# A written-out instruction sequence for each engine in place of ranked picks, and all bulk weights on one queue

## The chip, the core and the metric

The kernel runs on one core of a Trainium2 chip. What is measured is the device time of one execution, in microseconds (us). The core has five instruction streams that this kernel uses: TensorE (PE, with its weight loads PEld), VectorE (DVE), ScalarE (ACT), GpSimd (POOL) and SyncE (SP), which here only issues DMAs. Every stream runs its instructions strictly in order and waits on semaphores that the others raise.

## The reference

The input x has 2048 tokens of 448 features, in bf16. Two kinds of layer alternate, A, B, A, B, and each adds its result to x:

```python
x = x + _A_ref(_layernorm(x, axis=-1), A_wqkv, A_wo)
x = x + _B_ref(_layernorm(x, axis=-1), B_w_gate, B_w_up, B_w_down)
x = x + _A_ref(_layernorm(x, axis=-1), A_wqkv, A_wo)
x = x + _B_ref(_layernorm(x, axis=-1), B_w_gate, B_w_up, B_w_down)
```

A is attention with 16 heads of 28 features, in which each token sees 8 tokens: itself and those 2, 4 ... 14 places before it. The masked scores go through a softmax, and the result through the weight `wo`. B is a gated layer without a nonlinearity: (x w_gate) * (x w_up), 1792 features wide, and then w_down.

## The kernel before

**Data.** Tokens are taken with even ones first and odd ones second, so that a window of 8 tokens at distance 2 is a window of 8 neighbours. x stays in SBUF as 16 blocks of 128 tokens (`x_sb`). Layer 0 (A) works in five chunks of tokens (256, 512, 512, 512, 256), layer 2 (A) in four of 512, layers 1 and 3 (B) in five each. `SEQ` (line 74) lists the 19 jobs, "A00 A01 B10 A02 ...": the digits are layer and chunk. Later layers start on their first chunks while earlier ones still run.

**One chunk of A.** `ln_chunk` (line 762) makes the layernorm of each block: `bn`, `mv` on VectorE (L772, L774), `lnv`, `rstd` on ScalarE (L775, L777), `xn` on VectorE (L793); then the transpose T, by TensorE and an eviction (L803, L809) in layer 0 and by a DMA transpose from SP (L796) elsewhere. `qk_chunk` (line 863) makes q and k in four units, each with two PSUM banks, and evicts them (QK, L895); a copy of some rows goes through DRAM (`vt`, L904) to give v for four heads, which SP fetches with DMA transposes (VT, L915). `v_group` (line 917) makes the other heads' v. `attn_front` (line 993) makes the scores of two blocks of queries in one burst of 64 short matmuls (S, L1007; four banks), the exponentials on ScalarE (Ex, L1014) and the mask on VectorE (E, L1024). `attn_back` (line 1032) multiplies by v in another burst of 64 (AV, L1044; two banks), evicts (Oc, Oa, L1055, L1059) and normalises (Rs, Rl, R, N, L1069 to L1082). `y_blocks` (line 1086) multiplies by `wo` and adds to x (Y, x, L1099).

**One chunk of B.** `b_chunk` (line 1109) makes 14 units of gate and up (Gps; 14 matmuls each, two banks), evicts the gate on ScalarE (G, L1135), multiplies on VectorE (H, L1138) and then runs the down product (Dd) with another addition to x. The last two blocks have their own form (L1150, L1154), and their result goes out in three DMAs.

**PSUM** has eight banks; the queue of work for TensorE depends on when evictions free them.

**The order.** `Sched.add` (line 158) records every operation with the engines that may run it, an estimate of its time, what it depends on and which banks it takes or frees. `schedule` (line 281) then plays the program through with these estimates: whenever an engine is free, it picks among the operations that are ready by this plan the one with the lowest rank. The ranks are sums of tabled numbers by kind of operation and job (`PR`, `JP`, `XP`, lines 56 to 59, `HEAD_P`, `ATT_P`), with rules on when TensorE changes its tiling and how many banks each layer may hold (`HOLD_*`, `A_CAP`, `B_CAP`). An attention burst may be woven with up to two "strip" steps of a wide matmul that is also ready (lines 389 to 410, L537 in the profile). The plan also has estimates of how TensorE's code arrives (`LINE_T`, line 147). `emit` (line 456) writes each engine's instructions in the order found, with the semaphore waits that they need. The estimates set the order alone; on the chip each instruction runs when its waits are met.

**Loads.** Lines 647 to 660 load x, the q,k weights (four parts, `stg`) and the v weights, on the queues of SP and ACT. `bulk` (line 725) issues the large weights after x blocks 8 to 11 have landed: gate parts on SP and up parts on ACT (784 KB each), then `wo` in four parts and w_down in four, each of the latter waiting for the one before it.

Of the kernel before, what the change touches and what calls it, by code (L numbers as in the profile page):

```python
# [1 line left out]

# [7 lines left out]
S = 2048  # L10
D = 448
H = 16
DH = 28
# [14 lines left out]
MAIN = "R64"  # L28
# [5 lines left out]
HEAD_P = (38742.03, -267021.83, -101071.72, 99463.11, 27200.44)  # L34
HOLD_A = 14413.3
HOLD_BA = 5214.2
HOLD_BB = 9573.3
HOLD_N = 2
# [17 lines left out]
PR = {'wu': -168129.17, 'AV': -10462.61, 'rstd': -35978.42, 'bn': 17812.95, 'N': -10212.21, 'Gps': 180828.64, 'Tps': 27409.69, 'H': -109807.89, 'S': 144044.56, 'VT': 70347.33, 'Ex': 79610.91, 'G': -13543.26, 'xn': -79108.55, 'QK': -38047.91, 'Ddps': 24073.96, 'V': -99754.84, 'x': -42794.27, 'lnv': -73394.18, 'Oc': -92185.76, 'Oa': -11984.14, 'R': 151556.02, 'VVps': -36455.43, 'Yps': 17459.84, 'PW': 63857.07, 'T': -30210.14, 'mv': -55530.81, 'Rs': -97577.45, 'Rl': 77935.78, 'QKps': 68347.44, 'E': 103540.24, 'wqk': -93887.3, 'wqp': 55786.95}  # L56
JP = {'A20': -91058.29, 'B32': 33273.33, 'B34': -254788.12, 'A22': -140282.28, 'B13': -13087.65, 'A21': -140403.13, 'B12': -98678.01, 'A02': 51851.79, 'A03': -34167.99, 'B30': -93145.7, 'B31': 78379.27, 'B10': -36992.85, 'B11': -174975.04, 'A23': -71630.68, 'A04': 3260.23, 'B33': -59282.63, 'A01': -61687.66, 'B14': 99825.17, 'A00': -37201.99}
OFF = {}
XP = {'bn': -95955.38, 'mv': 16148.21, 'lnv': -72635.24, 'rstd': 84849.74, 'xn': -172701.07, 'Tps': 15935.95, 'T': 8483.92, 'QK': 48768.14, 'V': -165679.11, 'E': 31912.32, 'Ex': -27261.18, 'S': 103908.79, 'AV': -35522.85, 'Oc': 78601.92, 'Oa': -68237.35, 'N': 141909.88, 'x': -106916.56, 'VT': 41247.37, 'PW': -72014.64}
VONES_L = 6000.0  # L60
BL = (9000.0, 3500.0, 4000.0)
# [7 lines left out]
SEED = 190  # L69
JITTER = 0  # L70
ATT_P = 71709.67
A_CAP = 6
B_CAP = 6
# [59 lines left out]
class Sched:  # L133
# [13 lines left out]
    LINE_T = ((45000.0, 3500.0), (23000.0, 4600.0), (11000.0, 8500.0), (-1.0, 3500.0))  # L147

    def __init__(self):
        self.ops = []  # L150
        self.ready = {}
        self.fed = [(self.HEAD, 0.0)]
        self.lines = [0.0, 0.0]
        self.npos = 0
        self.met = {}
        self.rng = random.Random(SEED)

    def add(self, engs, ins, est, deps=(), prio=0.0, mode=None, acquire=None, release=(), dma=None, lat=0.0, after=None, selfd=(), tmin=None, alt=()):
# [7 lines left out]
        op.prio += JITTER * self.rng.random() + OFF.get(op.idx, 0.0)  # L166
        for _, k in ins:
            k = k[0] if isinstance(k, list) and k else k
            if isinstance(k, tuple) and k[0] in PR and k[0] != "cross" and not (dma and k[1] == -1):
                op.prio += PR[k[0]] + (XP.get(k[0], 0.0) if k[1] == 0 else 0.0)  # L170
                break
# [40 lines left out]
    def pick_banks(self, req, now):  # L212
# [14 lines left out]
        return cand[:req.n]  # L227

# [52 lines left out]
    def schedule(self):  # L281
# [13 lines left out]
        for op in self.ops:  # L295
# [9 lines left out]
            if not srcs:  # L305
                op.rdy = {x: self.ready_at(op, x) for x in op.engs}
                for e in op.engs:
                    pend[e].append(op)
        left = len(self.ops)
        now = 0.0  # L310
        while left:
            moved = False
            b_ready = any(o.acquire is not None and o.acquire.kind == 1 for o in pend["pe"])
            for e in self.ENGS:
                if free[e] > now + 1e-6:
                    continue
                best = None
                cands = []
                for op in pend[e]:
                    if op.rdy[e] <= now + 1e-6:  # L320
                        cands.append((op.prio, op.idx, op))
                cands.sort()
                a_wait = False
                okay = []
                for *_, op in cands:
                    if op.acquire is not None:
# [954 lines left out]
```

## Time and profile before

| | before |
|---|---|
| median of 3 runs | 390.56 us (389.87 to 390.77) |
| the profiled execution | 392.05 us |
| its span, first to last instruction | 390.3 us |
| busy: PE / DVE / ACT / POOL | 381.5 / 275.9 / 200.8 / 8.3 us |
| granted TensorE clock | 1.000 |
| DMA, mean over the span | 58 GB/s; 258, 263, 210 in the first three of 40 slices |

The profile is of one execution. Busy times count instructions of an engine that were running; a matmul's end is modelled from its size, so that a PE that waits a little between matmuls still looks busy. A "pair" below is two matmuls that use the upper and the lower 64 rows of the array at the same time: most of this kernel's matmuls come so. "Idle before, <- X" names what ended the wait of an engine; "issue" is a wait for nothing that the profile shows. In stretches of time, PE was busy as follows.

```profile
0.00:10.00 10.00, 8.74 (x86) 4.00 (x88) 6.17 (x16) 4.85 (x10) 7.22 (x32) 1.00 0.80 261
10.00:20.00 10.00, 9.38 (x192) 5.76 (x188) 9.77 (x33) 8.15 (x22) 0.00 (x0) 1.00 1.07 266
20.00:30.00 10.00, 9.21 (x279) 6.05 (x282) 7.63 (x23) 9.14 (x20) 1.09 (x6) 1.00 0.66 188
30.00:40.00 10.00, 9.86 (x147) 4.62 (x137) 6.79 (x17) 7.88 (x13) 0.00 (x0) 1.00 0.32 91
40.00:50.00 10.00, 9.05 (x319) 5.07 (x319) 7.14 (x17) 8.71 (x13) 0.00 (x0) 1.00 0.67 128
50.00:60.00 10.00, 8.25 (x207) 7.08 (x209) 8.45 (x18) 8.70 (x16) 0.00 (x0) 1.00 0.22 41
60.00:70.00 10.00, 10.00 (x221) 8.04 (x217) 10.00 (x27) 5.74 (x15) 0.00 (x0) 1.00 0.26 51
70.00:80.00 10.00, 9.18 (x284) 5.74 (x282) 8.04 (x23) 6.83 (x15) 0.00 (x0) 1.00 0.48 62
80.00:390.30 310.30, 307.85 (x4712) 167.41 (x4708) 211.93 (x441) 140.80 (x270) 0.00 (x0) 1.00 0.22 37
```

The columns are: the stretch, its length, busy us (and instructions) of PE, PEld, DVE, ACT and POOL, the granted clock, the DMA share and GB/s.

### The profile page before, as it was taken

The numbers are of one execution on the slowest core, as the hardware profiler recorded it, in microseconds if no ns is written. First come the engines' busy times: TensorE is split into PE (matmuls) and PEld (weight loads), VectorE is DVE, ScalarE is ACT, GpSimd is POOL, SyncE is SP. The second block draws the span as 40 slices with busy tenths as digits, with TensorE's granted clock in tenths as the row PEclk, the third lists the DMA queues.
The fourth block names the chain that finished last, engine by engine and source line by source line (L and its number), as shares of the span: only waits on it lengthen the run. The fifth ranks groups of instructions, "written<-read, shape, count | busy, mean of one in ns | idle before, by whom it ended". The sixth has DMA issues, their size and how long they took to land.

```text
span 390.3 us, 14405 instructions
## 1 busy us (share of the span) xinstructions
PE 381.5 (98%) x6394; PEld 213.8 (55%) x6394; DVE 275.9 (71%) x606; ACT 200.8 (51%) x386; POOL 8.3 (2%) x38
## 2 busy tenths in 40 slices
PE   8999989999999999999999999999999999999997
PEld 3555468554555544544456678545445544544584
DVE  6976789899649798496459965287676875467452
ACT  4797886664506676053544645055642542344150
POOL 7010000000000000000000000000000000000000
PEclk9999999999999999999999999999999999999999
DMA  7973532404302413221150204403230212100201
GB/s 258 263 210 92 131 41 56 58 11 83 41 2 53 61 21 50 49 29 29 22 55 15 41 13 33 82 26 52 37 64 29 40 34 50 50 2 2 51 23 47
DMA packets 54753, 22.50 MB, mean 58 GB/s; under 512 B 44884, under 2 KB 54692, under 8 KB 54692
## 3 DMA queue, kind: packets, MB, share of 16 engines
q1 hardware_dynamic: 53188, 19.24, 25.8%
q10 hardware_dynamic: 1504, 2.35, 2.2%
q8 instruction: 50, 0.82, 0.9%
q14 instruction: 11, 0.09, 0.1%
HBM read 8.54 MB, written 2.71 MB: 29 GB/s over the span
## 4 chain that ended last, share of the span: by engine, by line
PE 93%; ACT 4%; DVE 2%; issue 1%; ACTq 0%; DVEq 0%
PE ps L534 83%; PE ps L1007 3%; PE ps L1044 2%; PE ps L700 2%; PE ps L537 2%; PE ps L1150 1%; ACT qk L895 1%; ACT xnTa L809 1%; ACT E_sb L1014 1%; ACT R_sb L1070 0%; ACT g_sb L1135 0%; DVE oT L1082 0%; ACT O_sb L1055 0%; DVE v_sb L987 0%; DVE R_sb L1069 0%
## 5 line engine op out<-in xcount | busy, mean ns | idle before, releaser
L534 PE MATMUL ps<-xnTb,WGU 64*128 64x512 bf16 (+1 forms) x1942 | 176.8, 333 | 0.8 <-issue 0.8
L534 PEld LDWEIGHTS ps<-xnTb,WGU 64*128 64x128 bf16 x1942 | 94.2, 94 | 72.1 <-issue 1.5
L1135 ACT ACTIVATE g_sb<-ps 128x512 bf16<-128x512 f32 (+1 forms) x140 | 71.1, 511 | 92.9 <-PE ps L534 87.7
L1138 DVE TENSOR_TENSOR hT<-g_sb,ps 128x512 bf16<-128x512 bf16 (+1 forms) x140 | 79.6, 575 | 35.9 <-ACT g_sb L1135 34.0
L534 PE MATMUL ps<-WD,hT 64*128 64x448 bf16 x824 | 81.8, 349 | 0.0
L1099 DVE TENSOR_TENSOR x_sb<-x_sb,ps 128x448 bf16<-128x448 bf16 x62 | 35.9, 616 | 40.9 <-PE ps L534 40.8
L534 PEld LDWEIGHTS ps<-WD,hT 64*128 64x128 bf16 x824 | 39.6, 94 | 36.0
L534 PE MATMUL ps<-xnTa,WQK 64*128 64x512 bf16 (+1 forms) x488 | 51.6, 352 | 0.3 <-ACT xnTa L809 0.2
L1014 ACT ACTIVATE E_sb<-ps 128x1024 bf16<-128x1024 f32 (+1 forms) x36 | 33.7, 981 | 20.9 <-PE ps L1007 20.6
L772 DVE BATCH_NORM_STATS2 st<-x_sb 128x6 f32<-128x448 bf16 x64 | 37.4, 610 | 1.6 <-DMA x_sb<-in_A_x_dram 1.6
L793 DVE TENSOR_SCALAR xn_sb<-x_sb,mv,rstd 128x512 bf16<-128x512 bf16 (+1 forms) x64 | 34.1, 570 | 0.9 <-ACT rstd L777 0.8
L534 PEld LDWEIGHTS ps<-xnTa,WQK 64*128 64x128 bf16 x488 | 22.9, 94 | 20.5 <-ACT xnTa L809 1.1
L895 ACT ACTIVATE qk<-ps 128x1024 bf16<-128x1024 f32 (+1 forms) x30 | 26.9, 923 | 10.5 <-PE ps L534 10.3
L534 PE MATMUL ps<-wo_g,oT 64*128 64x448 bf16 x252 | 29.3, 349 | 0.1
L1024 DVE TENSOR_TENSOR E_sb<-E_sb,MK 128x1024 bf16<-128x1024 bf16 (+2 forms) x40 | 23.7, 608 | 7.2 <-ACT E_sb L1014 7.0
L1082 DVE TENSOR_TENSOR oT<-O_sb,R_sb 128x480 bf16<-128x480 f32 (+3 forms) x36 | 21.6, 627 | 5.2 <-ACT R_sb L1071 4.7
L1055 ACT ACTIVATE O_sb<-ps 128x512 f32<-128x512 f32 (+3 forms) x22 | 11.5, 547 | 26.4 <-PE ps L1044 26.3
L1070 ACT ACTIVATE R_sb<-R_sb 128x480 f32<-128x480 f32 (+1 forms) x34 | 20.0, 601 | 8.6 <-DVE R_sb L1069 8.5
L1069 DVE STREAM_SHUFFLE R_sb<-O_sb 128x480 f32<-128x480 f32 (+1 forms) x34 | 22.3, 696 | 0.0
L534 PE MATMUL ps<-WV,xnTa 64*128 64x336 bf16 (+3 forms) x244 | 21.1, 304 | 0.2
L1071 ACT ACTIVATE R_sb<-R_sb 128x480 f32<-128x480 f32 (+1 forms) x34 | 19.6, 601 | 0.4
L534 PEld LDWEIGHTS ps<-wo_g,oT 64*128 64x128 bf16 x252 | 12.5, 94 | 11.8 <-DVE oT L1082 1.1
(59 smaller groups left out, 190.7 us busy)
## 6 DMA issues: line engine op xcount, KB each, us to landing
out_dram<-x_sb SPq DMA_DIRECT2D x15, 112.0 KB, 1.7
WGU<-in_B_w_up_dram ACTq DMA_DIRECT2D x2, 784.0 KB, 11.5
WGU<-in_B_w_gate_dram SPq DMA_DIRECT2D x2, 784.0 KB, 13.5
x_sb<-in_A_x_dram SPq DMA_DIRECT2D x3, 448.0 KB, 7.1
WD<-in_B_w_down_dram SPq DMA_DIRECT2D x2, 448.0 KB, 3.8
hT<-in_A_wqkv_dram ACTq DMA_DIRECT2D x3, 224.0 KB, 3.5
WD<-in_B_w_down_dram SPq DMA_DIRECT2D x2, 336.0 KB, 3.9
vt<-qk SPq DMA_DIRECT2D x42, 16.0 KB
```

Source lines behind the costliest of these rows:

```text
L534: return lambda E: E.matmul(out(), lhs(), rhs(), start=start, stop=stop)
L772: sc.add("dve", one(lambda E, B=B: E.bn_stats(st6[:, B, :], x_sb[:, B, :]), ("bn", li, B)), 525.0, deps=[("x", li - 1, B)] + ([("xn", li - ...
L793: sc.add("dve", one(lambda E, B=B, dst=dst, src=src: E.tensor_scalar(dst, src, mv[:, B, 0:1], rstd[:, B:B + 1], ALU.subtract, ALU.mult), ( ...
L895: return E.activation(dst, src, ACT.Copy) if hasattr(E, "activation") else E.tensor_copy(dst, src)
L1014: return E.activation(E_sb[:, slot, 2 * hp:2 * hp + 2, 0:w], ps[:, b0:b0 + 2, 0:w], ACT.Exp, scale=SCALE)
L1024: return E.tensor_tensor(e, e, m, ALU.mult)
L1069: sc.add("dve", one(lambda E: E.stream_shuffle(R_sb[:, rs, 0:w], O_sb[:, os_, 0:w], [DH] * 32), ("Rs", li, qb)), dve_est(w) + 100.0, deps= ...
L1070: sc.add("act", one(lambda E: E.activation(R_sb[:, rs, 0:w], R_sb[:, rs, 0:w], ACT.Ln), ("Rl", li, qb)), act_est(w, False), deps=[("Rs", l ...
L1082: return E.tensor_tensor(oT[:, :, a % HALF:a % HALF + z - a], O[:, :, a - tok:z - tok], R_sb[:, rs, 0:w].rearrange("p (h n) -> p h n", h=4 ...
L1099: sc.add("dve", one(lambda E: E.tensor_tensor(x_sb[:, B, :], x_sb[:, B, :], ps[:, bk[w], 0:D], ALU.add), ("x", li, B)), dve_est(D), deps=[ ...
L1135: sc.add("act", one(lambda E, gs=gs, bk=bk: E.activation(g_sb[:, gs, 0:nt], ps[:, bk[0], 0:nt], ACT.Copy), ("G", li, j, fc)), act_est(nt), ...
L1138: sc.add("dve", one(lambda E, gs=gs, bk=bk, fc=fc: E.tensor_tensor(hT[:, fc, hs, 0:nt], g_sb[:, gs, 0:nt], ps[:, bk[1], 0:nt], ALU.mult), ...
```

## The change

`schedule` no longer ranks. A table `ORD` holds, for each engine, the numbers of the operations in the order in which that engine runs them (405 items for PE, 390 for ACT, 563 for DVE, 36 for POOL, 164 for SP); "a+b" is a burst woven with the wide matmul b. The play-through remains, to assign banks and to decide how a woven pair is cut, but it takes each engine's next item as given and waits until it is ready by the plan. The tables of ranks, the holding rules and the caps go. `LINE_T` and the estimated landing times of the weights change; these numbers reach the chip only through which banks are taken.

The computation and its matmuls are the same. Of the copies that ACT and DVE may both run (QK, V, T, Oc and a few others), 28 go from ACT to DVE and 28 from DVE to ACT; POOL takes all eight small weight copies of L717 (six before).

```diff
+    def banks_for(self, item, now):
...
+        given = {e: [tuple(map(int, x.split("+"))) for x in ORD[e].split()] for e in self.ENGS}
+        todo = {e: 0 for e in self.ENGS}
...
-                if best is None:
+                item = [self.ops[i] for i in given[e][todo[e]]]
+                if not all(op in pend[e] and op.rdy[e] <= now + 1e-6 for op in item):
                     continue
+                if not self.banks_for(item, now):
+                    continue
+                todo[e] += 1
...
-                if op.tmin is not None and e == "sp":
-                    gate = [o for o in self.pe_done if o.end + self.PE_LAT <= now and isinstance(o.ins[-1][1], tuple) and o.ins[-1][1] in self.ready]
-                    op.deps.append(gate[-1].ins[-1][1])
...
-    LINE_T = ((45000.0, 3500.0), (23000.0, 4600.0), (11000.0, 8500.0), (-1.0, 3500.0))
+    LINE_T = ((75000.0, 4300.0), (22000.0, 5300.0), (11000.0, 7700.0), (-1.0, 5000.0))
...
+    for j in range(4):
+        dst = wo_g[32 * j:32 * j + DH, :, :]
+        src = A_wo.rearrange("(c j e) d -> j e c d", c=4, j=4, e=DH)[j]
+        bulk("sp", dst, src, ("wo", j), f"d_wo{j}", BULK_AFTER, WOL)
+    lats = iter(BL)
     for n in range(2):
         f0, f1 = F // 2 * n, F // 2 * (n + 1)
         for m, (a, z) in enumerate(KP):
             for w, W_ in enumerate((B_w_gate, B_w_up)):
-                last = bulk(("sp", "act")[w], WGU[64 * w:64 * w + 64, a:z, f0:f1], W_[64 * a:64 * z, f0:f1].rearrange("(k p) f -> p k f", p=64), (("wg", "wu")[w], n, m), f"d_w{'gu'[w]}{n}{m}", BULK_AFTER, BL[0])
-    for j in range(4):
-        dst = wo_g[32 * j:32 * j + DH, :, :]
-        src = A_wo.rearrange("(c j e) d -> j e c d", c=4, j=4, e=DH)[j]
-        prev = bulk("sp", dst, src, ("wo", j), f"d_wo{j}", [last], BL[1])
+                prev = bulk("sp", WGU[64 * w:64 * w + 64, a:z, f0:f1], W_[64 * a:64 * z, f0:f1].rearrange("(k p) f -> p k f", p=64), (("wg", "wu")[w], n, m), f"d_w{'gu'[w]}{n}{m}", BULK_AFTER, next(lats))
```

Where the first 80 us differ most, in the names above (a name with two digits has layer and block, chunk or query block):

| engine | before | after |
|---|---|---|
| SP, first loads | x 0, x 1, stg 1, x 2-3, x 4-7, x 8-11, wv, x 12-15, stv | x 0, x 1, x 4-7, stg 1, x 2-3, x 8-11, wv, x 12-15, stv 1 |
| ACT, first loads | stg 0, 2, 3; later up 0, up 1 | stg 3, 2, 0 |
| SP, weights | gate 0, gate 1, wo 0-3, WD 0, then q,k copies, with WD 1, 2, 3 between them | wo 1, up 0, stv 0, wo 0, gate 0, up 1, wo 3, WD 0, WD 1, wo 2, WD 2, gate 1; WD 3 after VT 0.9 |
| SP, copies of chunks 2, 3, 4 | 4, 2, 3; VT 0.7 and 0.9 before those of chunk 3 | part of 4, part of 2, then 3 mixed with what is left of 2 and 4; VT 0.10, 0.8, 0.9 after them |
| ACT from 7 us | wqk 1, wqk 3, T 0.1, QK | wqk 0, T 0.0, wqk 1, T 0.1, ... QK |
| PE, second chunk of q,k | T 0.6 to T 0.9 within it | T 0.8, T 0.9 within it, T 0.6, T 0.7 after it |
| PE, around S 0.3 | ... T 10, T 11, QK unit, S 0.3, T 12, T 13, S 0.5 | T 10 to T 13 spread from AV 0.1 on; S 0.3, QK unit, Y and v work, S 0.5 |
| PE, AV 0.3 and AV 0.5 | woven with strips | not woven |
| PE, AV 0.11 | 17 items between S 0.11 and it | two gate/up units between S 0.11 and it, woven with a third |
| PE, chunks of B | units in order 0 to 13 | units in mixed order, down products of the chunk before among them |

More of the change, by code (lines that the diff above doesn't have):

```diff
@@ L1 @@
-import random
 import concourse.bass as bass
@@ L227, in pick_banks @@
         return cand[:req.n]
+    def banks_for(self, item, now):
+        held, ok = list(self.holder), True
+        for op in item:
+            if op.acquire is not None:
+                got = self.pick_banks(op.acquire, now)
+                if got is None:
+                    ok = False
+                    break
+                for b in got:
+                    self.holder[b] = op.acquire
+        self.holder = held
+        return ok
     def fed_at(self, i, ahead):
```

97 lines of the change are left out of this document (16 added, 81 removed), and 5 rows, old and new, of the table ORD.

## The prediction

> **What bounds the kernel now.** I read the page first.
>
> ```profile
> span 390.3 us, 14405 instructions
> ...
> PE 381.5 (98%) x6394; PEld 213.8 (55%) x6394; DVE 275.9 (71%) x606; ACT 200.8 (51%) x386; POOL 8.3 (2%) x38
> ...
> PEclk9999999999999999999999999999999999999999
> ...
> q8 instruction: 50, 0.82, 0.9%
> ```
>
> TensorE is the bound, at full clock, but its 98% hides waits. So I counted its 6394 matmuls by form and took each form's pitch (start to start of two pairs that follow each other in the trace): 216 ns a pair of 512 columns, 189 of 448, 142 of 336, 109 of 256, 10 ns an instruction in the short bursts of L1007 and L1044. Together 373.5 us; from the first matmul at 1.26 to the last end, 386.8 us pass. The 13.3 us between is all that an order can win. By stretch: 2.2 us in 0 to 10 (the warm-up at half pace), 1.7 in 10 to 20, 1.1 in 20 to 30, 0.4, 2.3, 1.4, 0.1, and 1.5 in 70 to 80; only 2.5 in the 310 us after 80. The new order has the same matmuls, so what counts is the first 80 us.
>
> Next, the chain of work that ended last, in order of time, around 50, 54 and 72 us.
>
> ```profile
> 49.87 0.09 PE ps L1044 x13
> 49.96 0.96 issue
> 50.92 0.22 PE ps L1044 x7
> ...
> 53.95 0.27 PE ps L534
> 54.21 0.77 issue
> 54.98 0.27 PE ps L534
> ```
>
> "issue" here waits for no engine. Queue 8 of the page carries instructions: 50 packets of 16 KB for TensorE's 12,930 recorded instructions, so 256 to a packet. The three gaps (0.96, 0.77, 0.77 at 71.77) stand before instructions 1985, 2241 and 3009, all 193 more than a multiple of 256; and the packets for these blocks landed at 49.53, 53.60 and 71.18, 1.35 to 1.38 us before TensorE went on. So TensorE waits for its own code there: **2.50 us**. From TensorE's reaching the block before until the next can run took 3.8, 4.1 and 5.3 us at the three; the same sum (packet start, its time, 1.37) gives 3.6 to 4.4 for eight of the other nine blocks before 80 us and 6.35 for one (705). A block with less work than that ends in a stall: the blocks ahead of the three gaps hold 2.79, 2.84 and 4.12 us by the pitches, because 73 to 93 of their 128 matmuls are short burst instructions.
>
> The timeline shows the third loss.
>
> ```profile
> 40.06 1.02 ACT L895 ACTIVATE qk<-ps 128x1024 bf16<-128x1024 f32 x1
> ...
> 40.99 1.93 ACT L1014 ACTIVATE E_sb<-ps 128x1024 bf16<-128x1024 f32 x2
> ...
> 41.15 0.29 PE L803 MATMUL ps<-ident,xn_sb 64*128 64x64 bf16 x8 [0.29 <-ACT qk L895]
> ...
> 42.06 0.33 PE L1007 MATMUL ps<-qk 28*64 28x64 bf16 x32 [0.62 <-ACT E_sb L1014]
> ```
>
> Two score bursts stand with two transposes alone between them; each takes four of the eight banks, so TensorE waits for the eviction of q,k and then the exponential: 1.26 us over pitch.
>
> **The change, part by part.**
>
> *Code blocks.* In the new sequence I cut TensorE's instructions (12,892: 12 matmuls and 14 waits fewer in this count) at the same places. The least block holds 4.14 us, the next 4.39 and 4.5; those ahead of the three gaps hold 4.59, 4.64 and 5.01. Against 3.6 to 4.4 none stalls; against the rare 5.3 or 6.35 a block of 4.1 to 5.1 loses 1 to 2 us. Two of the 12 blocks were that late; the waits that a block contains anyway lengthen it: I take 0.5 back, bounds 0 and 6 (rival A). Net **-2.0**.
>
> [...]
>
> *The crowding at 40 us.* Score burst S 0.5 now stands 30 matmuls (about 3.0 us at 100 ns each) behind S 0.3, longer than the two exponentials (1.93 us); the transposes of blocks 10 to 13 are spread over the q,k work from the burst AV 0.1 on. The 1.26 go. One transpose now stands 10 matmuls (1.1 us) behind AV 0.1 and wants a bank pair that is freed by an O eviction and an add (0.52 + 0.22 and some 0.8 of hand-overs): 0.5 is late. Net **-0.8**, bounds -1.3 and 0.
>
> *The head.* SyncE now loads x blocks 4 to 7 (448 KB) ahead of weight part 1 and x blocks 2, 3. Part 1 landed at 7.22 us; the bytes before it grow from 1120 to 1568 KB, which by the other landings (1344 KB by 7.89, 1792 by 9.08) is 8.5. ScalarE then does, in order, wqk 0, T 0.0, wqk 1, T 0.1, at 0.58 us each (L709 and L809 there), from 7.4 and with 8.5 before the third: 9.7. The first q,k matmul, at 8.82 now, waits for the last: 0.9 later. But TensorE then loses 2.9 us up to 25.2 (the chunk of 256 columns ran with 0.4 of filler in it; the waits at 12.9, 19.5, 23.2, 23.7 and 25.2 are 1.06, 0.37, 0.30, 0.52, 0.25 over pitch), and the new order changes these. ScalarE issues none of the gate and up weights (0.71 and 0.60 us of issue at 10.34 and 11.44), the 256-column chunk runs 9.7 to 12.75, its evictions and four transposes' evictions end on ScalarE near 15.9 (three of 0.6, then 0.55, 0.28, and three of 0.5, from 11.75), so the second q,k chunk starts near 16.0 (now 16.15). Its evictions have only T 8 and T 9 among them, one of four is VectorE's, and the last is done at 23.6, so that the third chunk starts near 24.45 instead of 25.16. **-0.7**, bounds -1.5 and +1.9 (the whole delay stays and the landing is a further 1.0 late).
>
> *Weights on one queue.* Each WD load waits for the one before, and the first for the up weights; gate part 2 stands behind WD 2. At the 247 GB/s with which the four WGU loads ran (3.2 MB from 13.6 to 26.6), the three ahead land by 24.5; WD 0 and 1 take 3.8 each by the page's rows, gate part 2 is issued near 33 and, at up to 11.5, lands by 45; its first reader runs near 58. Covered: **0**. Past the same queue go the v reorder DMAs: behind the last q,k eviction of chunk 3 stand 13 of them (7 now), at 2.96/7 = 0.42 us, then transposes of 1.4 us (5.64 for 4). VT 0.9, the third, lands 12.3 us after that eviction, the fourth WD load 15.1, VT 0.7 17.0; TensorE's own work until it needs them is 13.0, 16.1 and 18.1. Slack of about 1: 0 taken, bounds 0 and 1.5.
>
> *After 80 us.* 2.5 us are over pitch there, mostly 0.1 at each change of tiling; 31 strip groups woven for 29 changes little. VectorE is busy 18.5 of the 20 us from 80, and AV 0.11 now follows its scores after two units (3.0 us, the chain of two exponentials and a mask is 3.0): 0, bounds -0.8 and +2. The tail keeps its last three accumulations; the deferred output DMAs lie under them: 0.
>
> Sum: -2.0 - 0.8 - 0.7 = **-3.5 us**. The profiled execution took 392.05 (span 390.3, 1.75 around it), 1.5 over the median of 390.56; the difference goes on the median: **387.1 us** (span 386.8).
>
> **The rivals.** A difference under 0.2% (0.8 us) can't be told from none in this kernel.
>
> A. *Code comes late while the weights stream (slower).* Block 705 took 6.35 us at 260 GB/s. If the code of 961, 1217, 1473 and 1729 (behind 4.39, 5.05, 5.12 and 4.84 us of work) takes that too, the four lose 1.96 + 1.30 + 1.23 + 1.51 = 6.0; 1.0 of it lies over waits already counted and 0.5 I have counted: +4.5, so 391.6. It turns the sign from about 6.1 us a block. For: weights now stream without a pause from 10 to 45. Against: blocks 449 and 961, in the same traffic, took 3.8 and 4.3.
>
> B. *The gaps of code stay as they are.* They would follow TensorE's instruction count, not the density of bursts. Then -0.8 - 0.7 - 0: 389.1. Against: all three stand in the blocks with least work up to 80 us. [...]
>
> C. *The late head is not won back.* +1.9 in place of -0.7: 389.7. For: VectorE is busy 9.77 of 10 us from 10 to 20.
>
> D. *Fixed queues block.* VectorE and ScalarE take orders in which one late product holds all behind it; the 92% from 80 on is the place. At +2.0 there and 1.5 on the queue of SyncE: 390.6, no change.
>
> That the change doesn't do what it says is excluded: the two instruction sequences can be laid side by side.
>
> **Chances.** The forecast, between 1.5 and 6 us faster, 0.63; A 0.12; B 0.07; C 0.08; D 0.10. Faster: 0.63 + 0.07 + 0.08 (C, 0.9 us faster) = 0.78; within 0.2%: 0.09, most of D; slower: 0.13, A and the rest of D. Range: below, the best bounds of the first three terms (2.5 + 1.3 + 1.5) give 385.3, and most of the 0.8 after 80 makes it 384.7; above, it goes to 390.9, over B, C and D, and leaves out A.
>
> **What would show it.** Right: no "issue" of 0.7 us or more at 45 to 75 us; the first q,k matmul near 9.7 and the third q,k chunk near 24.5; the second of the two score bursts at 40 without a wait for E_sb; 80 to the end as long as before. Wrong: TensorE waiting before an instruction that is 193 above a multiple of 256 in the first 45 us (A); the same gaps (B); the third chunk after 26 (C); waits of L1044 for E_sb at 75 to 100, or for v_sb's DMA near 64 (D).

## The result and the profile after

| | before | after |
|---|---|---|
| median of 7 runs each | 390.64 us (389.87 to 391.92) | 393.80 us (392.02 to 395.04) |
| the profiled execution (its span) | 392.05 (390.3) us | 395.04 (393.3) us |
| granted TensorE clock in the profiled execution | 1.000 | 0.996 |

The ratio is 1.0073, interval 1.0049 to 1.0098: **slower by 0.7%**, where 0.9% faster was forecast. The page of the changed kernel:

```profile
span 393.3 us, 14306 instructions
...
PE 385.0 (98%) x6382; PEld 215.5 (55%) x6382; DVE 278.0 (71%) x603; ACT 194.7 (49%) x387; POOL 8.5 (2%) x40
...
PEclk9989999999999999999999999999999999999999
...
q8 instruction: 50, 0.82, 0.8%
```

PE looks 3.5 us busier with 12 matmuls fewer, and the clock row has an 8 where the kernel before has 9 throughout. TensorE's time over its pitches tells more: the time that passes less the sum of the pitches of its matmuls, counted as in the prediction (E13 is the best experiment below; us):

| stretch | before | after | E13 |
|---|---|---|---|
| 0 to 10 | 2.2 | 3.7 | 2.9 |
| 10 to 20 | 1.7 | 0.7 | 0.7 |
| 20 to 30 | 1.1 | 3.7 | 1.9 |
| 30 to 40 | 0.4 | 0.6 | 0.7 |
| 40 to 50 | 2.3 | 0.5 | 0.3 |
| 50 to 60 | 1.4 | 2.5 | 1.3 |
| 60 to 80 | 1.6 | 0.5 | 0.6 |
| 80 to the end | 2.5 | 4.1 | 3.6 |
| sum | 13.3 | 16.3 | 12.0 |

The 3.0 more are the difference of the spans. Up to 30 us the changed kernel loses 3.1, from 30 to 80 it gains 1.6, after 80 it loses 1.6.

What was forecast to go did go. The three gaps of 0.77 to 0.96 us for code are gone. In the chain of waits from 48 to 60 us no "issue" is longer than 0.05 us:

```profile
51.53 0.02 issue
...
54.82 0.02 issue
...
56.21 0.05 issue
56.26 0.90 PE ps L491 x7
```

In the timeline score burst S 0.5 (the second line with L964) starts without a wait, 3.8 us after S 0.3:

```profile
41.34 0.47 PE L964 MATMUL ps<-qk 28*64 28x64 bf16 x32
...
41.88 1.94 ACT L971 ACTIVATE E_sb<-ps 128x1024 bf16<-128x1024 f32 x2 [0.26 <-PE ps L964]
...
45.18 0.71 PE L964 MATMUL ps<-qk 28*64 28x64 bf16 x64
```

Two things are new. The head: the chain up to the first q,k matmul (10.60 us, before 8.82) is a weight chunk that lands at 8.51 and then ScalarE's four pieces of work in a row.

```profile
1.74 6.77 DMA hT<-in_A_wqkv_dram
...
8.53 0.58 ACT WQK L666
...
10.06 0.49 ACT xnTa L767
...
10.60 1.48 PE ps L491 x23
```

And the clock. This is the table by stretch (length, then busy us of PE, PEld, DVE, ACT, POOL, then the granted clock):

```profile
23.41:26.82 3.41, 2.15 (x134) 1.56 (x132) 2.47 (x8) 2.62 (x7) 1.83 (x10) 1.00 0.73 133
26.82:30.24 3.42, 3.36 (x38) 2.06 (x30) 1.12 (x2) 2.52 (x5) 0.00 (x0) 0.50 0.46 138
30.24:33.65 3.41, 3.41 (x118) 2.39 (x114) 2.46 (x6) 1.32 (x3) 0.00 (x0) 1.00 0.45 130
```

For 3.41 us TensorE runs at half clock. The 34 matmuls of 256 columns at 26.72 take 3.65 us, by their pitch 1.85: **1.8 us**. The 3.41 us ahead of it are thin: PE is busy for 2.15 of them, a share of 0.63; no such window of the kernel before, wherever it begins after 14 us, is under 0.72. TensorE waits there three times, twice for evictions and once for code, ahead of the third q,k chunk (the last line):

```profile
24.38 0.29 PE L761 MATMUL ps<-ident,xn_sb 64*128 64x64 bf16 x8 [0.15 <-DVE xnTa L767]
25.37 0.23 PE L964 MATMUL ps<-qk 28*64 28x64 bf16 x7 [0.70 <-ACT xnTa L767]
26.01 0.65 PE L964 MATMUL ps<-qk 28*64 28x64 bf16 x57 [0.41 <-issue]
...
26.72 4.46 PE L491 MATMUL ps<-xnTa,WQK 64*128 64x256 bf16 x40
```

In the trace the full clock begins at 6.342 us; the half clock comes 20.480 us later and lasts 3.413 us, so the full clock before it lasted six times as long. The window ahead of it was not idle: TensorE was busy for 0.63 of it. Of the seven runs two had full clock (392.0 and 393.0 us), five not (393.6 to 395.0). In the trace, every window of 3.41 us that begins between 22.36 and 24.82 us is under a share of 0.70. But 0.70 is not a threshold that these runs show: counted from the first full clock, the profiled run of E17 below has a window of 0.61 at 216 us, that of E16 one of 0.65 at 27 us, and the full clock stays in both.

### The profile page after: what moved, and what is told of

It is laid out like the page before. It is cut to its first block, busy times and chain, and to the rows that moved or that the text cites. A ratio compares the mean times of both kernels' runs of the same rounds, so it can differ in the third digit from the quotient of the medians.

```text
span 393.3 us, 14306 instructions
## 1 busy us (share of the span) xinstructions
PE 385.0 (98%) x6382; PEld 215.5 (55%) x6382; DVE 278.0 (71%) x603; ACT 194.7 (49%) x387; POOL 8.5 (2%) x40
## 3 DMA queue, kind: packets, MB, share of 16 engines
q1 hardware_dynamic: 54116, 20.85, 26.6%
## 4 chain that ended last, share of the span: by engine, by line
PE 87%; ACT 6%; DMA 3%; DVE 3%; issue 1%; SPq 1%; ACTq 0%
PE ps L491 80%; PE ps L964 2%; DMA hT<-in_A_wqkv_dram 2%; PE ps L1001 2%; PE ps L494 1%; PE ps L1107 1%; ACT xnTa L767 1%; DMA xnTb<-xn_sb 1%; ACT E_sb L971 1%; ACT qk L852 1%; SPq L872 1%; ACT g_sb L1092 1%; DVE xn_sb L751 1%; ACT O_sb L1012 1%; DVE oT L1039 0%
## 5 line engine op out<-in xcount | busy, mean ns | idle before, releaser
L1092 ACT ACTIVATE g_sb<-ps 128x512 bf16<-128x512 f32 (+1 forms) x140 | 68.9, 511 | 96.3 <-PE ps L491 87.4
L1095 DVE TENSOR_TENSOR hT<-g_sb,ps 128x512 bf16<-128x512 bf16 (+1 forms) x140 | 77.3, 575 | 38.2 <-ACT g_sb L1092 36.5
L491 PE MATMUL ps<-WD,hT 64*128 64x448 bf16 x820 | 83.8, 349 | 0.0
L491 PE MATMUL ps<-xnTa,WQK 64*128 64x512 bf16 (+1 forms) x488 | 53.3, 361 | 1.3 <-ACT xnTa L767 1.0
L751 DVE TENSOR_SCALAR xn_sb<-x_sb,mv,rstd 128x512 bf16<-128x512 bf16 (+1 forms) x64 | 35.4, 570 | 3.6 <-ACT rstd L735 3.6
L491 PEld LDWEIGHTS ps<-xnTa,WQK 64*128 64x128 bf16 x488 | 23.2, 97 | 22.2 <-ACT xnTa L767 2.1
L1027 ACT ACTIVATE R_sb<-R_sb 128x480 f32<-128x480 f32 (+1 forms) x34 | 20.4, 600 | 21.4 <-DVE R_sb L1026 21.4
L852 ACT ACTIVATE qk<-ps 128x1024 bf16<-128x1024 f32 (+1 forms) x24 | 21.4, 916 | 12.5 <-PE ps L491 12.4
L491 PE MATMUL ps<-WV,xnTa 64*128 64x336 bf16 (+3 forms) x252 | 23.1, 304 | 0.0
L733 ACT ACTIVATE lnv<-mv,eps_sb 128x2 f32<-128x2 f32 (+1 forms) x33 | 9.4, 293 | 23.0 <-DVE mv L732 20.4
L1028 ACT ACTIVATE R_sb<-R_sb 128x480 f32<-128x480 f32 (+1 forms) x34 | 20.5, 604 | 0.3
```

Source lines behind the costliest of these rows:

```text
L491: return lambda E: E.matmul(out(), lhs(), rhs(), start=start, stop=stop)
L751: sc.add("dve", one(lambda E, B=B, dst=dst, src=src: E.tensor_scalar(dst, src, mv[:, B, 0:1], rstd[:, B:B + 1], ALU.subtract, ALU.mult), ( ...
L852: return E.activation(dst, src, ACT.Copy) if hasattr(E, "activation") else E.tensor_copy(dst, src)
L1028: sc.add("act", one(lambda E: E.activation(R_sb[:, rs, 0:w], R_sb[:, rs, 0:w], ACT.Exp, scale=-1.0), ("R", li, qb)), act_est(w, False), de ...
L1092: sc.add("act", one(lambda E, gs=gs, bk=bk: E.activation(g_sb[:, gs, 0:nt], ps[:, bk[0], 0:nt], ACT.Copy), ("G", li, j, fc)), act_est(nt), ...
L1095: sc.add("dve", one(lambda E, gs=gs, bk=bk, fc=fc: E.tensor_tensor(hT[:, fc, hs, 0:nt], g_sb[:, gs, 0:nt], ps[:, bk[1], 0:nt], ALU.mult), ...
```

## The experiments

The changed kernel's matmuls and copies stay in all of them unless said; what moves are sequences. "Over pitch" is as above; "before" is the kernel before, run beside each group of experiments. Medians at full and at half clock are given apart where both occurred; of 128 runs of the kernel before beside these experiments, 4 had the half clock.

| run | median us | ratio to before (interval) | half clock | median at full / half clock |
|---|---|---|---|---|
| after | 393.80 | 1.0073 (1.0049 to 1.0098) | 5 of 7 | 392.5 / 393.8 |
| E1 | 393.57 | 1.0049 (1.0032 to 1.0067) | 0 of 6 | 393.6 / - |
| E2 | 391.84 | 1.0018 (0.9999 to 1.0037) | 3 of 12 | 391.5 / 393.5 |
| E3 | 392.92 | 1.0046 (1.0024 to 1.0068) | 6 of 12 | 391.7 / 394.4 |
| E4 | 393.80 | 1.0052 (1.0027 to 1.0077) | 5 of 7 | 391.8 / 394.3 |
| E5 | 391.66 | 1.0023 (1.0004 to 1.0043) | 6 of 12 | 390.8 / 392.6 |
| E6 | 397.37 | 1.0157 (1.0134 to 1.0179) | 4 of 5 | 395.7 / 397.4 |
| E7 | 398.25 | 1.0194 (1.0173 to 1.0215) | 4 of 4 | - / 398.3 |
| E8 | 397.82 | 1.0185 (1.0164 to 1.0207) | 4 of 4 | - / 397.8 |
| E9 | 392.98 | 1.0040 (1.0019 to 1.0061) | 0 of 12 | 393.0 / - |
| E10 | 393.26 | 1.0051 (1.0029 to 1.0073) | 1 of 12 | 393.2 / 395.3 |
| E11 | 392.20 | 1.0017 (0.9993 to 1.0041) | 0 of 12 | 392.2 / - |
| E12 | 391.91 | 1.0007 (0.9984 to 1.0030) | 0 of 12 | 391.9 / - |
| E13 | 390.43 | 0.9978 (0.9962 to 0.9994) | 0 of 12 | 390.4 / - |
| E14 | 393.36 | 1.0040 (1.0013 to 1.0068) | 4 of 12 | 392.8 / 394.2 |
| E15 | 391.48 | 1.0017 (0.9991 to 1.0043) | 3 of 12 | 391.4 / 394.1 |
| E16 | 391.20 | 1.0004 (0.9983 to 1.0024) | 1 of 12 | 391.1 / 393.9 |
| E17 | 393.75 | 1.0083 (1.0056 to 1.0110) | 1 of 6 | 393.7 / 396.4 |
| E18 | 390.79 | 1.0003 (0.9984 to 1.0023) | 4 of 12 | 390.2 / 392.3 |

### The half clock: E1

```diff
+                if (li, B) == (0, 14):
+                    for n in range(6):
+                        for h in range(2):
+                            ins.insert(0, (lambda E, h=h, bk=bk: E.matmul(ps[:, bk[h], 256:512], warm[64 * h:64 * h + 64, 0:128], warm[64 * h:64 * h + 64, 0:256], start=True, stop=True), None))
```

> The changed kernel with one thing added: twelve small matmuls on zeros (six pairs of 256 columns, about 0.65 us by the 109 ns that such a pair takes) in front of the transposes of token block 14, at 24.4 us, in the half of their PSUM banks that the transposes leave free. TensorE waits there until 25.4 us anyway, so nothing but its share of busy time changes. Theory: the half clock of 3.41 us from 26.8 us, which costs 1.8 us by the pitch of the 256-column run (3.65 us against 1.85 us), comes of the poorly filled window of 3.41 us ahead of it (TensorE busy for 0.63 of it, where no window of the kernel before falls under 0.72); filled to some 0.8, the clock stays at 1.0 in every run, and the median falls from 393.8 to 392.1 us, give or take 0.4 us. Rival, the half clock comes by chance or from something other than the gap: it stays in most runs and the median stays within 0.5 us of 393.8 us.

The half clock is gone from all six runs: it comes of the thin stretch (from 23.2 to 26.6 us TensorE is busy for 2.77 of 3.40 us in the profiled run, in the changed kernel for 2.14). The median did not follow. The 24 further instructions move every later edge between code blocks, and the profiled run shows 0.47 us of waiting for code at 25.3, 0.54 us over pitch before one at 246, and a wait of 0.66 us for an O_sb addition at 75: what the clock gave was lost elsewhere. E12 fills the same stretch (below) and has no half clock in twelve runs either.

### The first loads: E2

```diff
 SP: x 0, x 1
-x 4-7, stg 1, x 2-3
+stg 1, x 2-3, x 4-7
 DVE (and ACT alike): statistics
-of blocks 4, 5, then 3, 2
+of blocks 2, 3, then 4, 5
```

> The changed kernel with the first loads on the sync queue in the order of the kernel before (the second chunk of q and k weights, then token blocks 2 to 3, then 4 to 7), and the statistics of blocks 2 and 3 ahead of those of 4 and 5 on VectorE and ScalarE, so that nothing waits for the later load. Theory, the late first q,k matmul (10.60 against 8.82 us) is a late landing of the weight chunks (8.51 and 8.70 us) behind the token blocks: chunks land near 7.3 to 7.5 us, the first q,k matmul is at 9.4 to 9.7 us, 1 us earlier, and the median falls by 0.3 to 1.0 us to 392.8 to 393.5 us, less than the 1 us where the second chunk (17.0 us) or the third (26.7 us) waits for something else. Rival, the order of the conversions on ScalarE and of the transposes is what makes it late: first q,k matmul stays after 10.2 us and the median at 393.8 us.

The chunks landed at 7.10 and 7.28 us, the first q,k matmul was at 9.78 (forecast 9.4 to 9.7), the second chunk at 16.17, the third at 25.59: 0.8 us to 1.1 us earlier than in the changed kernel all along. At full clock the median is 1.0 us lower, but with only two such runs of the changed kernel to set against nine. E18 speaks against a whole microsecond.

### One queue: E3, E6, E11, E14

E3 puts the up weights back on ScalarE's queue in the changed order.

```diff
-SP: wo 1, up 0, stv 0, wo 0, gate 0, up 1, wo 3 ...
+SP: wo 1, stv 0, wo 0, gate 0, wo 3 ...    ACT: ... QK, up 0, T 2, up 1 ...
```

> The changed kernel with one part undone: the two loads of up weights go back from the sync queue to ScalarE's queue, at the places where the kernel before issues them. Rival theory, that the bulk weights on one queue cost the time: the median falls by 1 us or more towards 392.5 us. My theory, that the queue part costs nothing by itself and the order of single instructions does: 393.3 to 394.5 us; the two issues on ScalarE take some 0.5 to 0.8 us each there and can move an eviction at 17 to 20 us.

No clear gain: 0.9 us lower as a median, 0.8 us lower at full clock (against two runs), 0.6 us higher at half clock. Block 705's code came as late as in the changed kernel, 5.5 us after TensorE had reached the block ahead (5.4). E6 does the queue part alone, in the old order.

```diff
-SP: gate 0, gate 1, wo 0-3, WD 0 ...    ACT: ... up 0 ... up 1
+SP: gate 0, up 0, gate 1, up 1, wo 0-3, WD 0 ...
```

> The kernel before with the queue part of the change alone: the two loads of up weights on the sync queue, each right behind its gate weights, everything else in the old order. Theory, the queue part costs and gains nothing: within 0.5 us of the kernel before (390.9 us). Rival, that one queue delays the code blocks or the loads behind it: 391.5 us or more, with TensorE waiting at a code block or for a v_sb transpose.

The queue part alone costs 6.1 us in the old order (4.4 in the one run at full clock). The theory of no cost is wrong; the rival, 391.5 us or more with a wait at a code block, holds. The chain of waits at 28 us:

```profile
27.96 1.52 PE ps L491 x22
29.48 3.19 issue
32.67 0.39 PE ps L491 x4
```

"issue" again; the code block that starts there (instruction 961) came in a packet at 29.88 us, 5.29 us after TensorE had reached the block ahead of it. In the view of the DMA queues between 24.6 and 29.8 us there is no packet of queue 8; between 29.8 and 31.3 there is this one:

```profile
q8 instruction: 1, 0.02, 5.7%
```

Gate 1 landed at 26.59 and up 1 at 30.11 in that trace, so the code came with the end of the last weight load. In the changed kernel it was alike: block 705's packet started at 23.22 us, as gate 0 landed (23.28). E11 moves one load out of the way and nothing else:

```diff
-SP: gate 0, up 0, gate 1, up 1, wo 0-3, WD 0, copies of q,k chunk 4
+SP: gate 0, up 0, up 1, wo 0-3, WD 0, copies of q,k chunk 4, gate 1
```

> The sixth experiment (kernel before, all weights on the sync queue, 397.4 us) with one load moved: the second half of the gate weights goes behind the transfer of q,k chunk 4, past the four loads of output weights and the first of WD. All other engines' streams are the same, instruction for instruction. Theory, the 3.2 us that TensorE waits at 29.2 us is for a code block whose fetch (29.88 us, 5.3 us after the block ahead of it was reached) had to stand behind a weight load already queued (it comes out while the last of them lands, 28.6 to 30.1 us): with that load gone from there the fetch is at 25.5 to 27 us, the wait is under 0.5 us, and the median is 393.0 to 394.5 us. Rival, the fetch is late because the loads are on the sync queue at all: the wait stays over 2.5 us and the median over 396.5 us.

```profile
27.43 2.09 PE ps L491 x28
29.52 0.20 PE ps L1001 x21
```

The packet is at 26.47, 2.13 us after TensorE had reached the block ahead, the wait is gone from the chain, and 5.2 us come back (3.5 at full clock, against one run of E6), to below the 393.0 us at which the forecast began; all other engines run the same instructions. Block 705 is as late in E11 as in E6 and waits 0.8 us in both. So the code comes late **while weight loads are queued** (by 5.29 us in E6 with one queue, by 5.5 in E3 with two). E14 is the same from the other side, on E2: gate 0 is issued only when up 0 has landed.

```diff
+bulk(... gate 0 ...) with the wait for up 0
```

> The kernel of the second experiment with one wait more: on the sync queue the first gate weights are issued only when the first up weights have landed (18.5 us), so that no second weight load stands queued when TensorE's next code block is asked for at 17.0 us. Theory: the fetch of that block, at 22.1 us so far while the gate weights land (21.4 to 23.3 us), comes at 17.5 to 19.5 us, the wait for the block at 24.5 us (0.3 us) is gone, TensorE is busier in 23 to 26 us, and the half clock gets rarer (3 of 12 runs before). The loads behind it come some 2 us later, all before they are read. Median at full clock 391.2 us, 0.3 us less, 0.3 us either way. Rival, the fetch waits for something else than the load in front: it stays at 21 us or later and nothing changes but later weights, 391.5 us or more.

Half right. With nothing queued behind up 0 (landed 18.20), the code of block 705 came at 16.01 us, 0.08 us after TensorE reached the block ahead (E2: 22.11, 5.1 us after). But the loads are later, so the next block, 961, met gate 0 and up 1 (landed 24.95 and 28.96): packet at 28.31, a wait of 2.3 us in the chain, and a half clock in 4 of 12 runs, 1.3 us more than E2 at full clock. The collision moved by one block.

### Where the rest goes: sequences of one kernel up to a time, of the other after it

Here all five sequences are exchanged at a time of the plan, the seam:

```diff
 E4:  old order to 25 us, then new;  one queue
 E7:  old order to 30 us, then new;  loads as in E6
 E8:  E7 to 85 us, then old
 E9:  E7, but up 0 and up 1 on ScalarE's queue as before
 E10: E9 to 85 us, then old
 E5:  E2 to 85 us, then old
 E12: E5, with two pairs of zero matmuls ahead of the transposes of block 14
 E17: E13 to 208 us, then old
```

E4 was meant to price the head.

> The kernel before's sequences on all engines for the first 25 us or so (through the evictions of the second q,k chunk, the transposes of blocks 14 and 15 and the loads of the v weights), all that is left in the order of the changed kernel, with all bulk weights on the sync queue. Theory, head and half clock are the larger part of what was lost: the first q,k matmul is near 8.9 us and the third q,k chunk near 25.2 us, the clock stays at 1.0, and the median is 393.8 - 1.8 (half clock) - 1.5 (third chunk 26.7 to 25.2 us) = 390.5 us, as fast as the kernel before, give or take 0.8 us. Rival, the loss is in the later order and the head is won back by slack that the later stages have: 392.5 to 393.8 us.

It failed: its seam lay in the thin stretch, share 0.58, and five of seven runs had the half clock. E7 and E8 moved the seam to 30 us but carried the loads of E6, with 2.9 and 3.7 us of waiting for code at one block, so they say nothing of the order.

> The kernel before's sequences up to about 30 us on every engine (past the third q,k chunk's start), the changed kernel's order from there, weights on the sync queue. The seam now lies behind the thin stretch of TensorE at 24 us that gave the half clock to the fourth experiment. Theory, the head costs the changed kernel 1.8 us and the thin stretch the clock: no half clock, and by the profiles' sums after 30 us (changed kernel 9.0 us over pitch after 30 us, before 8.3 us, the head 5.0 us in the kernel before) 390.9 + 0.7 = 391.6 us, 0.5 us either way. Rival, the half clock comes with the changed order's loads and not with the thin stretch: half clock in most runs, 393 us or more.

> The seventh kernel up to about 85 us and the kernel before's sequences again from there, so that only the stretch of 30 to 85 us has the changed order. By the sums over pitch of the two profiles the changed order gains 1.8 us at 40 to 50 us and 1.1 us at 70 to 80 us and loses 1.0 us at 50 to 60 us and 0.2 us at 30 to 40 us: net -1.7 us, so theory expects 389.2 us, faster than both. Rival, the code-block and crowding gains are won back by waits at the seams or later: 390.5 to 391.5 us.

E9 and E10 mend that.

> The seventh experiment mended: the kernel before's sequences up to about 30 us on every engine, the up weights on ScalarE's queue as there, and the changed kernel's order from there on. Its predecessor waited 3.2 us for a code block at 29.6 us, which came of four weight loads one behind the other on the sync queue and says nothing of the order. Theory: no half clock and no late head, so what is left is the changed order's own balance after 30 us by the profiles (changed kernel 9.0 us over pitch, kernel before 8.3 us): 391.3 + 0.7 = 392.0 us, 0.6 us either way. Rival, the changed order after 30 us is better than before and only its head is at fault: 390.5 us or less.

> The ninth kernel up to about 85 us and the kernel before's sequences again from there: the changed order in 30 to 85 us alone, weights on two queues. By the sums over pitch (gains 1.8 us at 40 to 50 us and 1.1 us at 70 to 80 us, losses 1.0 us at 50 to 60 us and 0.2 us at 30 to 40 us) theory expects 391.3 - 1.7 = 389.6 us, less 0 to 1 us for the seams, at most 390.6 us. Rival, that the gains of the middle are lost at the seams and in later waits: 391 us or more.

E9: no half clock in twelve runs, first q,k matmul as before, and still 1.8 us slower than before. The gain at 40 to 50 us is there (0.3 over pitch against 2.3), but 2.3 stand at 50 to 60 (score bursts wait 0.3 us for an O_sb addition and 0.4 for v_sb, and one 0.6 for g_sb at 61.5), 1.2 at 70 to 80 (a wait of 1.0 us for an xnTb transpose at 79.5) and 0.5 at 296. E10: the middle alone gains 0.8 us by the stretches from 30 to 80, not 1.7, and gives it back ahead of 29.8 us (20 to 30 us is 1.1 over that of the kernel before, 0.7 of it a wait for a code block) and after the seam (1.2). A seam is a new order, and each brought waits of its own, so E5 and E17, which put the old order at the end, are bounds at best.

> The kernel of the second experiment (changed kernel with the first loads in the old order: 391.5 us median at full clock) up to about 85 us, and the kernel before's sequences for all that follows, on every engine. Theory, that the changed order loses 1.5 to 1.9 us after 80 us to waits of its own (the profile of the changed kernel has 4.4 us of TensorE time over pitch there, that of the kernel before 2.5 us; largest at 298 us, 0.7 us, and 243 to 250 us, 0.9 us): 389.6 to 390.4 us at full clock. Rival, TensorE's waits there depend on the moment at which the stage begins and not on the order: 391.0 to 392.0 us.

> The thirteenth kernel (390.4 us, all runs at full clock) up to about 208 us and the kernel before's sequences from there on. Theory, that the changed order still loses 0.5 us at 230 to 250 us (a code block that comes late at 245 us, 0.4 us) and 0.3 us at 270 us which the old order does not: 389.7 to 390.2 us. Rival, what is left there is run to run: 390.3 to 390.8 us.

E5: 0.7 us less than E2 at full clock, in spite of 1.1 us at its seam (a wait of 0.8 at 90 us), and 0.4 above the range that the theory gave. E17's seam at 208 us cost 3.7 us: inconclusive. E12 fills the stretch of E5.

> The fifth kernel (changed order with the old order of first loads, old order after 85 us: 390.8 us at full clock, 392.6 us in the half of its runs with the half clock) with four matmuls of 512 columns on zeros, about 0.43 us, ahead of the transposes of token block 14, as in the first experiment, but with 8 more instructions in place of 24. Theory: busy share of the worst 3.41 us window rises from 0.70 to some 0.8, no run shows the half clock, and the median falls from 391.7 to 390.8 us, 0.3 us either way, unless the 8 instructions bring a code block late (up to 0.8 us). Rival, the half clock stays in a third or more of the runs.

The clock part is right, the price wrong: 391.9. The same xnTb transpose came 0.9 us late at 78.5 us, and S waited 0.7 us for g_sb at 60.6.

### The order on the sync queue: E13, E15, E16, E18

```diff
 SP, on top of E2
-... stv 0 ...                T 1.0, 2 copies, T 1.1, ones, copies
+... stv 0, ones ...          T 1.0, T 1.1, copies
-VT 2.12, T 3.7, VT 2.15, T 3.6, VT 2.16, T 3.9, VT 2.13, VT 2.14, T 3.8
+VT 2.12, T 3.7, T 3.6, T 3.9, VT 2.13, VT 2.14, T 3.8, VT 2.15, VT 2.16
```

(The ones are a constant column that is written to vt once; GpSimd's memset of them also goes to the head.)

> The kernel of the second experiment (391.5 us at full clock, 393.5 us at half clock) with three moves on the sync queue alone; TensorE, ScalarE and VectorE run the same instructions. The copy of ones to the vt array goes back to the head (with its GpSimd memset), the second transpose of the first xnTb chunk goes right behind the first, ahead of two vt writes, and the transposes for blocks 13, 14 and 3.8 at 287 to 292 us go ahead of those for blocks 15 and 16. Theory: TensorE's wait for an xnTb transpose at 298 us (0.5 us) goes and its wait at 55 to 62 us (0.4 to 1.0 us) shrinks under 0.3 us: 0.5 to 1.2 us less, 390.3 to 391.0 us at full clock. Rival, the waits move to VectorE's products or to the next transposes: no change, 391.2 to 391.8 us at full clock. The half clock is left as it is.

390.43 us, 0.2% **under the kernel before** by an interval that leaves out 1, though at the limit of what the prediction held to be distinguishable, with all twelve runs at full clock; TensorE runs the changed kernel's instructions. Burst AV 2.13 needs the v transposes 2.13 and 2.14 and, for its woven unit of layer 3, the transpose T 3.8. In the changed kernel they stand on the sync queue behind 2.15 and 2.16 (issued at 286.60 and 290.23), and TensorE waits for the last:

```profile
292.85 2.51 SPq L872 DMA_TRANSPOSE v_sb<-vt  x2
295.41 1.30 SPq L754 DMA_TRANSPOSE xnTb<-xn_sb  x1
```

```profile
299.42 0.28 PE L1001 MATMUL ps<-E_sb,v_sb 64*32 64x64 bf16 x21 [0.50 <-DMA xnTb<-xn_sb]
```

In E13 T 3.8 (the first line) goes out ahead of 2.15 and 2.16 (the second), 5.6 us before the burst and not 4.0, and the burst does not wait:

```profile
289.47 1.30 SPq L754 DMA_TRANSPOSE xnTb<-xn_sb  x1
290.81 2.51 SPq L872 DMA_TRANSPOSE v_sb<-vt  x2
```

```profile
295.06 0.28 PE L1001 MATMUL ps<-E_sb,v_sb 64*32 64x64 bf16 x21
```

Over pitch, 290 to 300 us falls from 0.6 (E2) to 0.2 and 50 to 60 from 1.6 to 1.3, but the two waits of 0.3 and 0.4 us that E2 has there (for an O_sb addition and an oT product) stand in E13 too. Block 705's code came at 20.59 us instead of 22.11 and was not waited for.

> The last two kernels in one. Theory: 390.0 to 390.8 us, the half clock in at most a few runs; faster than the kernel before (391.1 us) by 0.3 to 1 us. Rival, the later weights delay the transfers of q,k to vt and the xnTb transposes behind them on the sync queue: over 391.5 us with a wait for xnTb at 55 us.

> The fifteenth kernel up to about 208 us and the kernel before's sequences from there on. Theory: the changed order's own waits at 230 to 250 us (0.9 us over pitch) and its late code block at 246 us go too, 0.5 to 1.0 us less than the fifteenth: 389.3 to 390.2 us, faster than both kernels. Rival, the seam at 208 us costs as much as the seam at 85 us did (1.1 us): no gain on the fifteenth.

E15 is E13 with E14's wait and is 0.9 us slower at full clock; TensorE stands 1.2 us ahead of block 961 in it. E16, with the old order from 208 us, is 0.3 us better than E15, within their spread. E18 has E13's moves without E2's:

```diff
-SP: x 0, x 1, stg 1, x 2-3, x 4-7     (E13)
+SP: x 0, x 1, x 4-7, stg 1, x 2-3     (as in the changed kernel)
```

> The changed kernel with the moves of the thirteenth run alone, its first loads left as the change has them. Theory, the late head (1.0 us) and the thin stretch at 24 to 26 us stay and the waits at 55 to 62 and 298 us go: full clock 391.4 us, half clock 393.0 us, the half clock in half of the runs or more, so a median of 392 to 393 us. Rival, that the head is won back once the later waits are gone: 390.8 us or less at full clock.

At full clock 390.2 us, 2.3 us under the changed kernel (two runs) and level with E13; as a median 390.8, level with the kernel before. All weights are still on one queue, in the changed order. So three moves on the sync queue (and the memset) make up for the loss, and the theory's price of 1.0 us for the load order is not borne out here. How they do it is shown in small part only. E18 and the changed kernel run the same TensorE instructions, and laid side by side the profiled E18 is ahead by 0.9 us at the first q,k matmul, 1.5 behind block 705's code, 2.6 at 32 us (the half clock), 2.9 at 43 (the code of 1473), 3.9 at 63, 4.1 at 250 and 4.5 from 299 us on. Only the last step is the wait that the moved transposes remove, and E2, without the moves, has the lead of 3.8 at 61 us too. The three moves were not tried apart. The head of the profiled run shows why it can vary: stg 0 landed at 7.62 us and the first q,k matmul stood at 9.71. With the same loads the changed kernel, E1 and E3 have landings at 8.51, 8.08 and 8.43 and first matmuls at 10.60, 10.17 and 10.52. With the old load order eight profiled runs of the new sequences (E2, E5, E12 to E17) spread from 8.58 to 10.04. What a load order fixes here is a spread, and one profile is one draw of it.

## Why the prediction was wrong

The forecast sum was -3.5 us; the profiled runs differ by +3.0. Up to 30 us it was +3.1 where -0.7 was forecast: the step that failed is the head, the third q,k chunk, and behind it the clock, which had no term. After 80 us it was +1.6 where 0 was forecast. (From the first matmul to the last end the trace of the kernel before has 386.65 us, not the 386.8 of the prediction; no term hangs on it.)

- **Code blocks** (-2.0): right in mechanism. The three gaps are gone; new waits for code end at 26.0, 43.3 and 249.5 us (instructions 705, 1473, 8897), 0.3 to 0.4 us each. Net about -1.4. The 1.37 us from a packet's landing to TensorE's going on came back as 1.2 to 1.6 at every stalled block of the profiled runs.
- **The crowding at 40 us** (-0.8): right, and larger: the 1.26 over pitch are gone and nothing is given back there.
- **The head** (-0.7): the steps up to the second chunk were right as far as the landing goes. Where stg 0 landed early (E18) the first q,k matmul was at 9.71 and the second chunk at 16.11, forecast 9.7 and 16.0. In the profiled run both were 0.9 to 1.0 late, and I had taken one landing as sure. The step that failed in every profiled run of the new order is the way to "the third chunk starts near 24.45", 14.75 us after the first q,k matmul: the chunk starts 15.6 to 16.1 us after it (E13, E14, E18; changed kernel and E12), and 16.7 in E3, because transposes of a block and S 0.1 stand ahead of it, which wait 0.9 us for evictions (0.15 and 0.70 in the lines above) and, in the changed kernel, 0.4 for code. In the profiled run that makes +1.6 at the third chunk, 26.72 for 25.16; of the 2.3 us beyond the forecast 0.9 are the landing and 1.4 this. By its sign, the third chunk after 26 us, rival C came about, near its +1.9.
- **The clock** had no term at all. A sum by pitches takes full clock for granted; the thin stretch that the late third chunk leaves brought +1.8 us in the profiled run, and 1.3 to 2.8 us between the medians of one kernel's runs at full and half clock.
- **Weights on one queue** ("Covered: 0", "0 taken"): wrong in what it left out. I looked at when each load and each v transpose is read. I left out what comes late with queued loads without being an instruction of SP (TensorE's code) and two other orders on the queue: the ones and the copies around T 1.1, and the transposes of layer 3 near 295 us. Undoing the move of the weights brought no clear gain (E3); undoing these orders made the kernel level with the one before (E18). In the profiled run 0.5 us at 299 is seen to come of them and 0.4 at 26 of the late code; the rest is not traced to a wait. Rival A named the first, at 0.12, and asked for 6.1 us a block; 705 took 5.41 + 1.40 + 1.39 = 8.2 us in the changed kernel but stood behind enough work that only 0.4 us showed. A's sign, waits at code blocks in the first 45 us, came twice, at 26.0 and 43.3. E6 shows the price in the old order: 6 us, the half clock of four of its five runs included.
- **50 to 60 us and after 80** ("0"): +1.1 and +1.6 by the table; with the code gap that went from 50 to 60, the order's own waits there are +2.0. In E13 the first is 1.2 less and the second 0.5, but E2 already has 0.9 of the 1.2. E9 shows that the changed order is not better than the old after 30 us; which of its waits is dear differs from run to run, and that remains open.

Rival D said that fixed queues block, at 390.6 us. It was near in kind; its place (VectorE from 80 us) was not the one, and its second place (SP) was one of several.

Settled: the half clock comes of the thin stretch (E1, E12, the windows); code comes late while weight loads are queued (E6, E11, E14: 5.29, 2.13 and 0.08 us after TensorE reached the block ahead); with other DMA orders on SP alone, and the order of four statistics, the new sequences are at least level with the kernel before (E13, E18). Of the eighteen times that the theories gave, only E13's held; what they said of single waits, packets and the clock held more often. Open: how the three moves of E18 act and which of them does; what the 56 copies that changed engine are worth, since they were in every run of the new order; and at what share, if at any, the clock halves. By busy time, 0.55 to 0.70 brought it in a quarter to five sevenths of the runs of E2 to E5 and the changed kernel, 0.74 (E12) in none; 0.73 in 4 of 12 runs of E18 and none of E13, and E10 and E16 with 0.65 only once each. With the windows of E16 and E17 above, busy time by the profile does not settle it.

## What to carry to other kernels

When an order is changed by hand, look at the queue of DMAs first: TensorE's own code can come late while large loads are queued (5.29 us after the block ahead was reached in E6), and one load moved (E11, 5.2 us) was worth more than any reordering of matmuls here. A stretch in which TensorE is only two thirds busy can cost more than its gaps: in the changed kernel a share of 0.63, with waits of 0.15, 0.70 and 0.41 us, was followed by 3.41 us at a clock of 0.50, which cost 1.8 us. Price a head by the spread of its landings, not by one profile.

## What was not expected of the hardware

- The half clock began 20.480 us after the first full clock of the run in the changed kernel, E3 and E4, and 27.307 us after it in E7, E8 and E14: six and eight times the 3.413 us for which it lasted in the changed kernel.
- A 16 KB code packet came 0.08 us after TensorE reached the block ahead of it with nothing queued behind the load under way (E14), and 5.3 us after, as the last load landed, with loads queued (E6). These runs don't show when the fetch is asked for, so whether it is asked for late or has to wait stays open. Weights are not the only cause: in the kernel before, block 3009's packet came 2.8 us after (70.05 us), with no weight load under way.
- Twelve matmuls put into a wait removed the half clock and moved the edges of all later code blocks by 24 instructions, and the median stayed within 0.3 us (E1).
